# A new plan for layer two's weight pairs inside layer one of a retention and two-MoE kernel

## The chip, the cores and the metric

One core of a Trainium2 chip runs the whole program in one launch. The metric is the device time of an execution in microseconds; the median of three runs of the kernel before is 853.76 us (853.73 to 854.74).

## The reference, cut to what matters

```python
scores = scale * np.matmul(q, k.transpose(0, 1, 3, 2))          # 4 x 8 heads, 576 x 576, head 64
ret = scores * Dmat[None]                                        # decay gamma ** (i - j), causal
x = np.matmul(ret, v).transpose(0, 2, 1, 3).reshape(2304, 512)
h = x @ w_in;   g = np.maximum(h, 0) + alpha * np.minimum(h, 0)  # layer one, d_ff 2048
x = g @ w_out
h = x @ w_in2;  g = h * (1 / (1 + np.exp(-1.702 * h)))           # layer two, d_ff 2048
return g @ w_out2
```

The weights arrive as 64-bit floats, two 32-bit words each, and are turned into 32-bit floats on the chip. Each operand of a matmul is split into a rounded high part and the rest (hi and lo), and three products (hi hi, hi lo, lo hi) replace one.

## The kernel before, in words

There are three stages. Retention comes first (L228 to L346 of the kernel). Layer one follows: the 2304 tokens are cut into five chunks (`CH`, four of 512 columns, number 4 of 256), and the work is a list of 80 steps, numbered 0 to 79 here. One step takes one chunk and one tile of 128 hidden features: `mm1` (L394) makes h with 12 matmuls, ScalarE and VectorE make g from it (`activate`: two ACT passes L404 and L405, one DVE pass L406), `split` writes g's high part on ACT (L84, by `copy`) and its low part on DVE (L87, by `sub`) into `gsf`, and `mm2` (L437) adds the product with the second weight into four banks of PSUM, acc0 to acc3. TensorE's order is mm1(i), mm2(i - 2), mm1(i + 1), and so on. Steps 0 to 31 do chunks 0 and 1 in five blocks, 32 to 47 chunk 2, 48 to 63 chunk 4, 64 to 79 chunk 3. When a chunk ends, its four acc banks are copied out (L458 on DVE, L84 on ACT), and the next chunk's first mm2 writes the same banks. The next chunk's input is loaded (L376, tile xf) and split into x ahead of the change by `x_load` and `x_split`.

Layer two follows in three rounds. It is a scheme with 7 products of blocks in place of 8, a product being one unit (L558, 6 matmuls of 384 columns). Before round 0 it needs x2 (`x2_load`, `x2_steps`: four sums, seven splits for each of k = 0 and 1) and `ws` (split by `r_split` from `rw`). Its 16 weight tiles are converted in eight pairs (j = 0 to 7) during layer one, which `pair_words` plans. A pair is

- for each of its two tiles: the load of raw words (L110, two halves of 512 KB), `w_abs` (ACT, L114), `w_clamp` (DVE, L118 and L121), `w_top` (DVE, L128), `w_low` (DVE, L135), which turn tile raw into tile cv;
- `sums1` and `sums2` (DVE, L465, four sums of 128x256 each);
- `r_store`, five DMAs into rg in DRAM (L178 to L182);
- for seven blocks in three groups: `b_hi` (ACT, L84, rounds a half of the block in place), `b_lo` (DVE, L197), `b_store` (two DMAs into sg in DRAM, L201).

The places of tiles make waits. There are two buffers of cv and two of raw. `b_hi` overwrites what `r_store` reads, so it waits until that DMA has landed. `w_abs` of the next pair overwrites what `b_store` reads, so it waits for that. All DMAs are issued by SP, in program order.

The order is written by hand: every piece of work is put on a list with a time (`at`), and `run_to` emits what is due between the pieces of a step. All engines run what they were given in order. The times of the pairs are microseconds since the start of layer one; `tick` turns them into steps by what TensorE takes for a step without waits.

```python
    def tick(us):
        i = max(n for n in range(n_s) if begins[n] <= us)
        return base + i + (us - begins[i]) / (begins[i + 1] - begins[i])
```

Of the kernel before, what the change touches and what calls it, by code (L numbers as in the profile page):

```python
# [7 lines left out]
F32 = mybir.dt.float32  # L8
# [21 lines left out]
R, RN = 3, 384  # L30
# [2 lines left out]
BANK = "abcabcb"  # L33
GSRC = (0, 4, 1, 3, 0, 2, 3)
NG = 5


@with_exitstack
def kernel(
# [12 lines left out]
    nc = tc.nc  # L52
# [5 lines left out]
    def pool(name, bufs, **kw):  # L58
        return ctx.enter_context(tc.tile_pool(name=name, bufs=bufs, **kw))
# [4 lines left out]
    xp = (pool("xp", 1), pool("xq", 1))  # L64
# [16 lines left out]
    sg = [[dram.tile([128, 4, 2, 256], F32, name=f"sg_{i}_{h}") for h in range(2)] for i in range(7)]  # L81
# [10 lines left out]
    def at(time, fn, *args):  # L92
        events.append((time, len(events), fn, args))

    def run_to(time):
        while events and events[0][0] <= time:
            _, _, fn, args = events.pop(0)
            fn(*args)


    wt, raws, cvs, x_t, sums = {}, {}, {}, {}, {}
    both = "p (c n) -> p c n"

    def w_load(key, src, slot):
# [48 lines left out]
    def quarter(j, e, c):  # L153
        return cvs[2, 2 * j + e][:, c * 256:c * 256 + 256]

    def sums1(j, home):
        if home < 2:
            t = cvp.tile([128, 2, 4, 256], F32, tag=f"raw{home}", name="sums")
            t = [t[:, g] for g in range(2)]
        else:  # L160
            t = [xp[0].tile([128, 4, 256], F32, tag=f"x{2 + g}", name="sums") for g in range(2)]
        sums[j] = t
        m = [[quarter(j, e, c) for c in range(2)] for e in range(2)]
        add(t[0][:, 1], m[1][0], m[1][1])
# [19 lines left out]
    def block2(j, i):  # L184
        if i in (1, 2, 4, 5):
            n = {1: 0, 2: 1, 4: 2, 5: 3}[i]
            return sums[j][0][:, n], sums[j][1][:, n]
        e, h, l = {0: (0, 3, 2), 3: (1, 0, 2), 6: (1, 1, 3)}[i]
        return quarter(j, e, h), quarter(j, e, l)
# [7 lines left out]
        nc.vector.tensor_tensor(out=f.bitcast(F32R), in0=f, in1=hi, op=ALU.subtract)  # L197

    def b_store(j, i):
        for c, t in enumerate(block2(j, i)):  # L200
            nc.sync.dma_start(out=sg[i][j // 4][:, j % 4, c], in_=t)  # L201

    def pair_words(j, t0, t1, l0, l1, slots, home):
        for e, (t, ld) in enumerate(((t0, l0), (t1, l1))):
            key = 2, 2 * j + e
            at(tick(ld), w_load, key, w2, slots[e])
            at(tick(ld) + 0.01, w_piece, key, w2, 1)
            for fn, d in ((w_abs, 0.0), (w_clamp, 2.0), (w_top, 3.6), (w_low, 5.2)):
                at(tick(t + d), fn, key)
        t = t1 + 7.8  # L210
        at(tick(t), sums1, j, home)
        at(tick(t + 1.0), r_store, j)
        at(tick(t + 1.6), sums2, j)
        t += 2.0
        for g, blocks in enumerate(((0, 3), (6, 1), (2, 4, 5))):
            for i in blocks:
                at(tick(t + 2.8 * g), b_hi, j, i)
                at(tick(t + 2.8 * g + 2.8), b_lo, j, i)
                at(tick(t + 2.8 * g + 4.2), b_store, j, i)


    ld, r_t, k_t, s_t, sc_t, av_t, xs_t = {}, {}, {}, {}, {}, {}, {}
# [142 lines left out]
    acc = [None]  # L365
# [118 lines left out]
    def x2_load(r, k):  # L484
        for h in range(2):
            if r:
                t = cvp.tile([128, 2, RN], F32, tag="cv", name="xr", bufs=2)
            else:
                t = xp[0].tile([128, 2, RN], F32, tag=f"x{2 * k + h}", name="xr")
            xr[k, h] = t  # L490
            f = t.rearrange("p c n -> p (c n)")
            for c, (c0, c1) in enumerate(CH):
                s0, s1 = max(c0, r * 2 * RN), min(c1, r * 2 * RN + 2 * RN)
                if s0 < s1:
                    nc.sync.dma_start(
                        out=f[:, s0 - r * 2 * RN:s1 - r * 2 * RN],
                        in_=x1[c][:, 2 * h + k, s0 - c0:s1 - c0],
                    )
# [22 lines left out]
    def x2_steps(k, t, step, gap):  # L521
        for i in range(7):
            for phase in range(3):
                at(t + step * i + gap * phase, x2_step, k, i, phase)
# [21 lines left out]
        t = ws["s", n] = wp.tile([128, 4, 2, 256], F32R, tag=f"w{6 + n % 5}", name="ws2")  # L546
        nc.sync.dma_start(out=t.bitcast(F32), in_=sg[i][h])

    def new_bank(what, n):
        tag = {"a": f"acc{n}", "b": "h", "c": f"acc{2 + n}"}[what]  # L550
        t = mps.tile([128, 512], F32, tag=tag, name=tag, bufs=4 if what == "b" else 1)
        return t[:, 0:RN]

    def product(out, pairs, start):
        n = 0
        for w, x in pairs:
            for cw, cx in ((0, 0), (1, 0), (0, 1)):
                nc.tensor.matmul(  # L558
                    out=out, lhsT=w(cw), rhs=x(cx), start=(start and n == 0), stop=True,
                    skip_group_check=True,  # L560
                )
                n += 1

    def unit1(j, i):
        b = BANK[i]
        new = i < 3 or b == "b"
        if new:
            bank[b] = new_bank(b, j % 2)
        w = ws[2 * j + i // 4][:, :, i % 4]
        product(  # L570
            bank[b],
            [
                (lambda c, k=k: w[:, c, k * 128:k * 128 + 128], lambda c, k=k: xblk(i, k, c))
                for k in range(2)
            ],
            new,
        )
# [100 lines left out]
    for m, t in enumerate(pace):  # L678
        d = 0.75 if m < 3 else 0.5
# [3 lines left out]
    for i in range(n_a):  # L683
        b = PAIRS[i][0]
# [7 lines left out]
    with tc.manual_schedule():  # L692
# [47 lines left out]
        n1 = base + n_s  # L740
        homes = {c: xp[c] for c in range(2)}
        for n, (_, c, m0, _) in enumerate(BLOCKS[N_FIRST:], 1):
            homes[c] = xp[n % 2]
            for k in range(NK):
                t = starts[c, m0] - (4 if n == 1 else 6) + (0.9 if n == 1 else 1.3) * k
                at(t - 1.6, x_load, c, k)
                at(t, x_split, c, k, xp[n % 2])
        for c, n, t in ((0, 0, 17), (1, 1, 25.5), (0, 2, 30)):
# [14 lines left out]
        )):  # L763
            pair_words(j, *plan)
        x2_steps(0, n1 - 7.2, 0.4, 0.5)
        at(n1 - 8.4, x2_load, 0, 0)
        x2_steps(1, n1 - 2.4, 0.4, 0.5)
        at(n1 - 3.2, x2_load, 0, 1)
        for n in range(3):
            at(n1 - 1.5, r_load, n)  # L770
        for n in range(2):
# [24 lines left out]
        for r in range(R):  # L796
# [41 lines left out]
        for u in range(R * 2 * NU):  # L838
            r, v = divmod(u, 2 * NU)
            if v < NU:  # L840
                unit1(*divmod(v, 7))
            else:
                unit2(v - NU)
            run_to(u + 1)
# [60 lines left out]
```

## Time and profile before

| | |
|---|---|
| median of 3 runs | 853.76 us |
| the profiled execution, its own time | 855.07 us |
| its span in the profile | 853.3 us |
| retention, about | 0 to 83.6 us |
| layer one, first mm1 to the last mm2 | 83.6 to 495.97 us |
| layer two, first unit | 498.59 us |
| DVE and ACT busy, share of the span | 74% and 54% |

Times inside the profile count from the start of its span. In a timeline row, several instructions of one kind are merged; the bracket at its end is the idle time of the engine ahead of it and what ended it.

### The profile page before, as it was taken

The numbers are of one execution on the slowest core, as the hardware profiler recorded it, in microseconds if no ns is written. First come the engines' busy times: TensorE is split into PE (matmuls) and PEld (weight loads), VectorE is DVE, ScalarE is ACT, GpSimd is POOL, SyncE is SP. The second block draws the span as 40 slices with busy tenths as digits, with TensorE's granted clock in tenths as the row PEclk, the third lists the DMA queues.
The fourth block names the chain that finished last, engine by engine and source line by source line (L and its number), as shares of the span: only waits on it lengthen the run. The fifth ranks groups of instructions, "written<-read, shape, count | busy, mean of one in ns | idle before, by whom it ended". The sixth has DMA issues, their size and how long they took to land.

```text
span 853.3 us, 14011 instructions
## 1 busy us (share of the span) xinstructions
PE 830.4 (97%) x5132; PEld 755.2 (88%) x5132; DVE 633.2 (74%) x1128; ACT 457.9 (54%) x920; POOL 0.2 (0%) x4
## 2 busy tenths in 40 slices
PE   8999999999999999899998989999999999999998
PEld 7888888888888888798786879999999999999998
DVE  2997796777485587666767678779877799677875
ACT  4643665554353445445435566666566566566553
POOL 0000000000000000000000000000000000000000
PEclk8999999999999999899999999999999999999999
DMA  7985742454156563754554544498544787544872
GB/s 264 324 310 184 250 170 99 151 193 173 35 202 214 173 208 101 235 186 136 204 194 140 190 162 128 150 340 293 198 139 130 264 296 268 178 122 173 295 275 81
DMA packets 66548, 166.97 MB, mean 196 GB/s; under 512 B 7600, under 2 KB 33840, under 8 KB 60720
## 3 DMA queue, kind: packets, MB, share of 16 engines
q1 hardware_dynamic: 66480, 166.08, 57.0%
q8 instruction: 40, 0.66, 0.3%
q14 instruction: 28, 0.23, 0.1%
HBM read 128.83 MB, written 37.22 MB: 195 GB/s over the span
## 4 chain that ended last, share of the span: by engine, by line
PE 77%; DVE 9%; DMA 6%; ACT 4%; issue 3%; SPq 1%; DVEq 0%; ACTq 0%
PE acc L558 24%; PE h L558 18%; PE h L394 15%; PE acc L437 15%; PE av L262 3%; DMA raw<-in_w_dram 2%; DMA sg<-cv 2%; DVE sums L465 1%; PE st L262 1%; PE sc L262 1%; DMA rg<-sums 1%; DVE g L406 1%; DVE cv L118 1%; ACT cv L114 1%; DVE cv L128 1%
## 5 line engine op out<-in xcount | busy, mean ns | idle before, releaser
L437 PE MATMUL acc<-gsf,w 128*128 128x512 f32 (+1 forms) x960 | 216.0, 374 | 9.9 <-DVE o L458 5.2
L394 PE MATMUL h<-x,w 128*128 128x512 f32 (+1 forms) x960 | 211.7, 370 | 0.0
L437 PEld LDWEIGHTS acc<-gsf,w 128*128 128x128 f32 x960 | 170.4, 192 | 44.6 <-DVE gsf L87 6.6
L84 ACT ACTIVATE gsf<-g 128x384 fp32r<-128x384 f32 (+2 forms) x248 | 132.8, 543 | 120.0 <-DVE g L406 77.4
L394 PEld LDWEIGHTS h<-x,w 128*128 128x128 f32 x960 | 169.3, 190 | 30.8 <-DVE w L87 0.7
L87 DVE TENSOR_TENSOR gsf<-g,gsf 128x384 fp32r<-128x384 f32 (+2 forms) x248 | 141.5, 580 | 51.2 <-ACT gsf L84 49.7
L558 PE MATMUL acc<-x,ws 128*128 128x384 f32 x576 | 112.2, 336 | 2.6 <-DVE o L458 2.6
L406 DVE SCALAR_TENSOR_TENSOR g<-h,nalpha_sb,g 128x512 f32<-128x512 f32 (+1 forms) x80 | 55.6, 695 | 72.5 <-ACT h L405 72.2
L558 PEld LDWEIGHTS acc<-x,ws 128*128 128x128 f32 x576 | 101.5, 189 | 3.0 <-ACT ws L84 3.0
L558 PE MATMUL acc<-gsf,ws 128*128 128x384 f32 x576 | 101.3, 334 | 0.0
L558 PEld LDWEIGHTS acc<-gsf,ws 128*128 128x128 f32 x576 | 100.0, 188 | 0.0
L558 PE MATMUL h<-x,ws 128*128 128x384 f32 x432 | 87.4, 337 | 0.0
L558 PEld LDWEIGHTS h<-x,ws 128*128 128x128 f32 x432 | 76.8, 190 | 0.0
L558 PE MATMUL h<-gsf,ws 128*128 128x384 f32 x432 | 76.3, 334 | 0.0
L558 PEld LDWEIGHTS h<-gsf,ws 128*128 128x128 f32 x432 | 75.0, 188 | 0.0
L404 ACT ACTIVATE g<-h 128x512 f32<-128x512 f32 (+1 forms) x80 | 43.7, 547 | 49.9 <-PE h L394 49.8
L465 DVE TENSOR_TENSOR tm<-h,tm 128x384 f32<-128x384 f32 x72 | 40.0, 555 | 35.8 <-PE h L558 31.5
L87 DVE TENSOR_TENSOR ws<-rw,ws 128x512 fp32r<-128x512 f32 x96 | 57.0, 616 | 0.0
L465 DVE TENSOR_TENSOR g<-g,g 128x384 f32<-128x384 f32 x93 | 51.4, 553 | 0.7
L84 ACT ACTIVATE ws<-rw 128x512 fp32r<-128x512 f32 x96 | 49.8, 569 | 0.0
L114 ACT ACTIVATE cv<-raw 128x1024 f32<-128x1024 f32 x32 | 36.1, 1128 | 17.5 <-DMA raw<-in_w_dram 13.9
L405 ACT ACTIVATE h<-h 128x512 f32<-128x512 f32 (+1 forms) x80 | 44.0, 550 | 0.0
(70 smaller groups left out, 687.5 us busy)
## 6 DMA issues: line engine op xcount, KB each, us to landing
ws<-sg SPq DMA_DIRECT2D x42, 1024.0 KB, 6.8
raw<-in_w_dram SPq DMA_DIRECT2D x64, 512.0 KB, 4.9
ld<-in_qkv_dram SPq DMA_DIRECT2D x15, 864.0 KB, 6.7
rw<-rg SPq DMA_DIRECT2D x24, 512.0 KB, 3.5
rw<-rg SPq DMA_DIRECT2D x24, 384.0 KB, 3.1
sg<-sums SPq DMA_DIRECT2D x64, 128.0 KB, 2.0
sg<-cv SPq DMA_DIRECT2D x48, 128.0 KB, 3.0
kts<-in_kn_dram SPq DMA_DIRECT2D x16, 256.0 KB, 6.9
```

Of the source, the lines that this page charges most:

```text
L84: return nc.scalar.activation(out=out, in_=in_, func=ACTF.Copy)
L87: return eng.tensor_tensor(out=out, in0=a, in1=b.bitcast(F32), op=ALU.subtract)
L114: nc.scalar.activation(out=cvs[key], in_=raws[key][:, :, 1].bitcast(F32), func=ACTF.Abs)
L118: nc.vector.tensor_scalar(out=f, in0=f, scalar1=F64_MIN, scalar2=F64_MAX, op0=ALU.max, op1=ALU.min)
L262: nc.tensor.matmul(out=out, lhsT=lhsT, rhs=rhs, start=start, stop=stop, skip_group_check=True)
L394: nc.tensor.matmul(out=t, lhsT=w[:, cw, k * 128:k * 128 + 128], rhs=x[:, cx], start=(i == 0), stop=(i == 3 * NK - 1),)
L404: nc.scalar.activation(out=g, in_=t, func=ACTF.Relu)
L405: nc.scalar.activation(out=t, in_=t, func=ACTF.Relu, scale=-1.0)
L406: nc.vector.scalar_tensor_tensor(out=g, in0=t, scalar=nalpha_sb[:, m:m + 1], in1=g, op0=ALU.mult, op1=ALU.add)
L437: nc.tensor.matmul(out=acc[0][d], lhsT=w[:, cw, d * 128:d * 128 + 128], rhs=g[:, cx], start=(m == m0 and i == 0), stop=(m == m1 - 1 and i ...
L465: nc.vector.tensor_tensor(out=out, in0=x, in1=y, op=op)
L558: nc.tensor.matmul(out=out, lhsT=w(cw), rhs=x(cx), start=(start and n == 0), stop=True, skip_group_check=True,)
```

## The change: what it does

It changes the plan's numbers and rules in `pair_words`, the homes of a few tiles, the form of some stores, and the banks of layer two's first pair.

- `PAUSES`: `tick` adds 10, 9 and 11 us to a plan time that reaches 176, 261 and 309 us. Pair work is thus planned around the three ends of chunks. The table of the pairs has new times, for the words (t0, t1) and the loads (l0, l1).
- Inside a pair the steps are closer: the words' pieces at 0, 1.6, 3.0, 4.4 us (0, 2.0, 3.6, 5.2 before), sums at t1 + 6.2 (7.8), the groups of blocks 2.4 us apart (2.8).
- Loads of the next pair's words are planned after `r_store` of the pair before it.
- The sums of pair 4 live in tiles x2 and x3 of pool xq (`home` 3), those of pair 5 in raw1; pair 6 stays in pool xp. x2's raw input `xr` for k = 1 is loaded into x0 and x1, as for k = 0, and no longer into x2 and x3. k = 0 begins 0.8 step earlier, k = 1 1.0 step earlier, and its load 1.2 step earlier.
- Blocks 3 and 6 are stored by one DMA with two runs per partition, and so are blocks 1, 2, 4, 5 where the sums lie in one tile.
- x of chunks 4 and 3 is split 4.4 steps (6 before) ahead of their first step, 0.9 step apart (1.3).
- In pair j = 0 of round 0, layer two's banks a and c come from the four buffers of h and no longer from acc.

```diff
+PAUSES = ((176, 10), (261, 9), (309, 11))
...
-            t = [xp[0].tile([128, 4, 256], F32, tag=f"x{2 + g}", name="sums") for g in range(2)]
+            t = [xp[home - 2].tile([128, 4, 256], F32, tag=f"x{2 + g}", name="sums") for g in range(2)]
...
     def b_store(j, i):
-        for c, t in enumerate(block2(j, i)):
-            nc.sync.dma_start(out=sg[i][j // 4][:, j % 4, c], in_=t)
+        dst = sg[i][j // 4][:, j % 4]
+        if i in (3, 6):
+            f = cvs[2, 2 * j + 1].rearrange("p (a b n) -> p a b n", a=2, b=2)
+            nc.sync.dma_start(out=dst, in_=f[:, :, i // 6])
+        elif i and j in whole:
+            nc.sync.dma_start(out=dst, in_=whole[j][:, :, {1: 0, 2: 1, 4: 2, 5: 3}[i]])
...
-            for fn, d in ((w_abs, 0.0), (w_clamp, 2.0), (w_top, 3.6), (w_low, 5.2)):
+            for fn, d in ((w_abs, 0.0), (w_clamp, 1.6), (w_top, 3.0), (w_low, 4.4)):
...
-                t = xp[0].tile([128, 2, RN], F32, tag=f"x{2 * k + h}", name="xr")
+                t = xp[0].tile([128, 2, RN], F32, tag=f"x{h}", name="xr")
...
-        tag = {"a": f"acc{n}", "b": "h", "c": f"acc{2 + n}"}[what]
+        tag = "h" if ring else {"a": f"acc{n}", "b": "h", "c": f"acc{2 + n}"}[what]
...
-                t = starts[c, m0] - (4 if n == 1 else 6) + (0.9 if n == 1 else 1.3) * k
+                t = starts[c, m0] - (4 if n == 1 else 4.4) + 0.9 * k
...
+            for begin, length in PAUSES:
+                us += length if us >= begin else 0
...
-            (320, 334, 312, 327, (1, 0), 2), (349, 357, 328, 342, (1, 0), 2),
+            (296, 307, 289, 300, (0, 1), 2), (322, 328, 304.5, 316, (0, 1), 2),
...
-        x2_steps(0, n1 - 7.2, 0.4, 0.5)
-        at(n1 - 8.4, x2_load, 0, 0)
-        x2_steps(1, n1 - 2.4, 0.4, 0.5)
-        at(n1 - 3.2, x2_load, 0, 1)
+        for k in range(2):
+            at(n1 - 9.0 + 4.6 * k, x2_load, 0, k)
+            x2_steps(k, n1 - 8.0 + 4.6 * k, 0.4, 0.5)
```

In the changed kernel the lines after the inserted ones have moved: L465 is L473 there, L406 is L414, L458 is L466, L87 is L88, L135 is L136, L110 is L111, L178 to L182 are L180 to L184.

SP, about step 47 to 49, where pair 3's results are stored and pair 4's words loaded (rg_101 belongs to pair 4). Before:

```order
L110 DMA raw<-in_w_dram 128x1024 x2
L178 DMA rg_100<-cv 128x256
L179 DMA rg_100<-cv 128x256
L180 DMA rg_100<-cv 128x256
L181 DMA rg_100<-sums 128x512
L182 DMA rg_100<-sums 128x512
L201 DMA sg_0_105<-cv 128x256 x2
L201 DMA sg_0_111<-cv 128x256 x2
```

and now:

```order
L180 DMA rg_100<-cv 128x256
L181 DMA rg_100<-cv 128x256
L182 DMA rg_100<-cv 128x256
L183 DMA rg_100<-sums 128x512
L184 DMA rg_100<-sums 128x512
L111 DMA raw<-in_w_dram 128x1024 x2
L210 DMA sg_0_105<-cv 128x256 x2
L205 DMA sg_0_111<-cv 128x2x256
```

The 1 MB load has moved from ahead of the five stores into rg to behind them, and so ahead of the stores into sg; block 3's store is one DMA.

VectorE (DVE) at the end of chunk 2, from g of step 47 to the copy of acc0 and acc2 (COPY o). Before:

```order
L406 SCALAR_TENSOR_TENSOR g<-h,nalpha_sb,g 128x512
L87 TENSOR_TENSOR gsf<-g,gsf 128x512
L197 TENSOR_TENSOR cv<-cv 128x256 x2
L406 SCALAR_TENSOR_TENSOR g<-h,nalpha_sb,g 128x256
L197 TENSOR_TENSOR cv<-cv 128x256
L197 TENSOR_TENSOR sums<-sums 128x256
L87 TENSOR_TENSOR gsf<-g,gsf 128x256
L406 SCALAR_TENSOR_TENSOR g<-h,nalpha_sb,g 128x256
L458 COPY o<-acc_2447 128x512
L458 COPY o<-acc_2449 128x512
```

and now:

```order
L414 SCALAR_TENSOR_TENSOR g<-h,nalpha_sb,g 128x512
L199 TENSOR_TENSOR sums<-sums 128x256 x3
L88 TENSOR_TENSOR gsf<-g,gsf 128x512
L119 TENSOR_SCALAR cv<-cv 128x1024
L122 TENSOR_SCALAR cv<-cv 128x1024
L414 SCALAR_TENSOR_TENSOR g<-h,nalpha_sb,g 128x256
L88 TENSOR_TENSOR gsf<-g,gsf 128x256
L414 SCALAR_TENSOR_TENSOR g<-h,nalpha_sb,g 128x256
L466 COPY o<-acc_2438 128x512
L466 COPY o<-acc_2440 128x512
```

Pair 3's `b_lo` (cv<-cv and sums<-sums) now ends in step 47; only pair 4's first `w_clamp` stands in step 48, and nothing of a pair between it and the copies.

VectorE in step 74, the fullest 512-column step after the change (x, xr, xs belong to `x2_steps`, cv and sums to pair 7). Before:

```order
L118 TENSOR_SCALAR cv<-cv 128x1024
L121 TENSOR_SCALAR cv<-cv 128x1024
L87 TENSOR_TENSOR x_4129<-xr,x_4129 128x384
L128 SCALAR_TENSOR_TENSOR cv<-raw,cv 128x1024
L465 TENSOR_TENSOR xs<-xr 128x384
L406 SCALAR_TENSOR_TENSOR g<-h,nalpha_sb,g 128x512
L135 SCALAR_TENSOR_TENSOR cv<-raw,cv 128x1024
L87 TENSOR_TENSOR x_4148<-xr,x_4148 128x384
L87 TENSOR_TENSOR gsf<-g,gsf 128x512
```

and now:

```order
L122 TENSOR_SCALAR cv<-cv 128x1024
L88 TENSOR_TENSOR x_4109<-xr,x_4109 128x384
L129 SCALAR_TENSOR_TENSOR cv<-raw,cv 128x1024
L473 TENSOR_TENSOR xr<-xs,xr 128x384
L414 SCALAR_TENSOR_TENSOR g<-h,nalpha_sb,g 128x512
L136 SCALAR_TENSOR_TENSOR cv<-raw,cv 128x1024
L88 TENSOR_TENSOR x_4087<-xs,x_4061 128x384
L473 TENSOR_TENSOR xr<-xr,xs 128x384
L473 TENSOR_TENSOR sums<-cv 128x256
L473 TENSOR_TENSOR sums<-sums,cv 128x256
L473 TENSOR_TENSOR sums<-cv 128x256
L473 TENSOR_TENSOR sums<-cv,sums 128x256
```

(One `w_clamp` row stands ahead of these, and gsf 128x512 ends the step.) The four sums and one x2 operation have come into this step from step 75.

## Rows read from the trace of the kernel before

**Rows 1.** The page: busy time by engine, and the granted clock in 40 slices.

```profile
PE 830.4 (97%) x5132; PEld 755.2 (88%) x5132; DVE 633.2 (74%) x1128; ACT 457.9 (54%) x920; POOL 0.2 (0%) x4
...
PEclk8999999999999999899999999999999999999999
```

**Rows 2.** TensorE's timeline, steps 48 to 52: start, length, line, wait ahead.

```profile
339.15 1.60 PE L394 MATMUL h<-x,w 128*128 128x256 f32 x12
...
353.37 2.90 PE L437 MATMUL acc<-gsf,w 128*128 128x256 f32 x12 [3.44 <-DVE o L458]
...
360.40 1.60 PE L394 MATMUL h<-x,w 128*128 128x256 f32 x12
361.84 1.60 PE L437 MATMUL acc<-gsf,w 128*128 128x256 f32 x12
```

**Rows 3.** TensorE's timeline, steps 60 to 67, the change from chunk 4 to 3.

```profile
383.44 1.60 PE L394 MATMUL h<-x,w 128*128 128x256 f32 x12
...
397.67 2.91 PE L394 MATMUL h<-x,w 128*128 128x512 f32 x12
...
410.67 3.01 PE L437 MATMUL acc<-gsf,w 128*128 128x512 f32 x12 [1.73 <-DVE o L458]
413.51 2.88 PE L394 MATMUL h<-x,w 128*128 128x512 f32 x12
416.23 2.88 PE L437 MATMUL acc<-gsf,w 128*128 128x512 f32 x12
```

**Rows 4.** TensorE's timeline, step 74 to layer two's fifth unit.

```profile
458.46 4.09 PE L437 MATMUL acc<-gsf,w 128*128 128x512 f32 x10 [2.67 <-DVE gsf L87]
...
484.14 2.88 PE L394 MATMUL h<-x,w 128*128 128x512 f32 x12
...
498.59 1.62 PE L558 MATMUL acc<-x,ws 128*128 128x384 f32 x6 [2.62 <-DVE o L458]
...
504.40 1.20 PE L558 MATMUL h<-x,ws 128*128 128x384 f32 x6
505.44 1.20 PE L558 MATMUL acc<-x,ws 128*128 128x384 f32 x6
```

**Rows 5.** All engines' timeline ahead of the wait in rows 2 (SPq: DMA issues).

```profile
340.36 0.81 SPq L110 DMA_DIRECT2D raw<-in_w_dram  x2
...
346.99 0.42 ACT L84 ACTIVATE cv<-cv 128x256 fp32r<-128x256 f32 x1 [1.84 <-DMA rg<-cv]
...
348.34 0.42 ACT L84 ACTIVATE sums<-sums 128x256 fp32r<-128x256 f32 x1 [0.93 <-DMA rg<-sums]
...
352.54 1.28 DVE L458 COPY o<-acc 128x512 f32<-128x512 f32 x2
```

**Rows 6.** DMA issues by tiles: count, KB each, median us from issue to landing.

```profile
sg<-sums SPq DMA_DIRECT2D x64, 128.0 KB, 2.0
...
rg<-cv SPq DMA_DIRECT2D x24, 128.0 KB, 5.6
```

**Rows 7.** All engines' timeline ahead of the two waits in rows 4.

```profile
450.52 1.14 ACT L114 ACTIVATE cv<-raw 128x1024 f32<-128x1024 f32 x1 [1.26 <-DMA sg<-cv]
...
486.80 0.56 DVE L465 TENSOR_TENSOR xr<-xr 128x384 f32<-128x384 f32 x1 [4.42 <-DMA xr<-x]
...
497.75 1.28 DVE L458 COPY o<-acc 128x512 f32<-128x512 f32 x2
```

**Rows 8.** VectorE by line and form, 260 to 500 us: busy us, mean ns | idle before.

```profile
L406 DVE SCALAR_TENSOR_TENSOR g<-h,nalpha_sb,g 128x512 f32<-128x512 f32 x31 | 23.2, 748 | 30.4 <-ACT h L405 30.4
...
L135 DVE SCALAR_TENSOR_TENSOR cv<-raw,cv 128x1024 int32<-128x1024 int32 x14 | 17.1, 1220 | 0.2
L465 DVE TENSOR_TENSOR sums<-cv 128x256 f32<-128x256 f32 x28 | 11.7, 418 | 0.0
L121 DVE TENSOR_SCALAR cv<-cv 128x1024 int32<-128x1024 int32 x14 | 9.7, 694 | 0.5
L87 DVE TENSOR_TENSOR x<-xr,x 128x384 fp32r<-128x384 f32 x12 | 6.6, 553 | 0.0
```

More of the change, by code (lines that the diff above doesn't have):

```diff
@@ L98, in run_to @@
             fn(*args)
-    wt, raws, cvs, x_t, sums = {}, {}, {}, {}, {}
+    wt, raws, cvs, x_t, sums, whole = {}, {}, {}, {}, {}, {}
     both = "p (c n) -> p c n"
@@ L158, in sums1 @@
             t = cvp.tile([128, 2, 4, 256], F32, tag=f"raw{home}", name="sums")
+            whole[j] = t
             t = [t[:, g] for g in range(2)]
         else:
-            t = [xp[0].tile([128, 4, 256], F32, tag=f"x{2 + g}", name="sums") for g in range(2)]
+            t = [xp[home - 2].tile([128, 4, 256], F32, tag=f"x{2 + g}", name="sums") for g in range(2)]
         sums[j] = t
@@ L199, in b_store @@
     def b_store(j, i):
-        for c, t in enumerate(block2(j, i)):
-            nc.sync.dma_start(out=sg[i][j // 4][:, j % 4, c], in_=t)
+        dst = sg[i][j // 4][:, j % 4]
[4 more added lines that the diff above has]
+            nc.sync.dma_start(out=dst, in_=whole[j][:, :, {1: 0, 2: 1, 4: 2, 5: 3}[i]])
+        else:
+            for c, t in enumerate(block2(j, i)):
+                nc.sync.dma_start(out=dst[:, c], in_=t)
     def pair_words(j, t0, t1, l0, l1, slots, home):
@@ L207, in pair_words @@
             at(tick(ld) + 0.01, w_piece, key, w2, 1)
-            for fn, d in ((w_abs, 0.0), (w_clamp, 2.0), (w_top, 3.6), (w_low, 5.2)):
+            for fn, d in ((w_abs, 0.0), (w_clamp, 1.6), (w_top, 3.0), (w_low, 4.4)):
                 at(tick(t + d), fn, key)
-        t = t1 + 7.8
+        t = t1 + 6.2
         at(tick(t), sums1, j, home)
-        at(tick(t + 1.0), r_store, j)
-        at(tick(t + 1.6), sums2, j)
-        t += 2.0
+        at(tick(t + 0.9), r_store, j)
+        at(tick(t + 1.5), sums2, j)
         for g, blocks in enumerate(((0, 3), (6, 1), (2, 4, 5))):
             for i in blocks:
-                at(tick(t + 2.8 * g), b_hi, j, i)
-                at(tick(t + 2.8 * g + 2.8), b_lo, j, i)
-                at(tick(t + 2.8 * g + 4.2), b_store, j, i)
+                at(tick(t + 1.8 + 2.4 * g), b_hi, j, i)
+                at(tick(t + 4.2 + 2.4 * g), b_lo, j, i)
+                at(tick(t + 5.4 + 2.4 * g), b_store, j, i)
     ld, r_t, k_t, s_t, sc_t, av_t, xs_t = {}, {}, {}, {}, {}, {}, {}
@@ L547, in s_load, with new_bank @@
         nc.sync.dma_start(out=t.bitcast(F32), in_=sg[i][h])
-    def new_bank(what, n):
-        tag = {"a": f"acc{n}", "b": "h", "c": f"acc{2 + n}"}[what]
-        t = mps.tile([128, 512], F32, tag=tag, name=tag, bufs=4 if what == "b" else 1)
+    def new_bank(what, n, ring=False):
+        tag = "h" if ring else {"a": f"acc{n}", "b": "h", "c": f"acc{2 + n}"}[what]
+        t = mps.tile([128, 512], F32, tag=tag, name=tag, bufs=4 if tag == "h" else 1)
         return t[:, 0:RN]
@@ L562, in product, with unit1 @@
                 n += 1
-    def unit1(j, i):
+    def unit1(r, j, i):
         b = BANK[i]
@@ L567, in unit1 @@
         if new:
-            bank[b] = new_bank(b, j % 2)
+            bank[b] = new_bank(b, j % 2, r + j == 0)
         w = ws[2 * j + i // 4][:, :, i % 4]
@@ L840 @@
             if v < NU:
-                unit1(*divmod(v, 7))
+                unit1(r, *divmod(v, 7))
             else:
```

6 rows, old and new, of the table i are left out of this document.

## The prediction

> **What bounds the kernel now.** I read the page first: TensorE (PE) is busy 97% of the span, DVE 74%, ACT 54%, and past its first slice the granted clock shows one dip, in the 17th of 40 slices, 341 to 363 us [rows 1]. So TensorE sets the end, and a change that adds no matmul and removes none can only win back what TensorE loses to waits and to a lower clock. Then I went down TensorE's timeline through layer one and compared starts with the undisturbed pace. That pace is 1.44 us for 12 matmuls of 256 columns (360.40 to 361.84, [rows 2]), 2.72 us for 12 of 512 (413.51 to 416.23, [rows 3]) and 1.04 us for a unit of layer two (504.40 to 505.44, [rows 4]). Up to step 48 the starts keep it. From there to layer two's fifth unit they do not, and the losses fall into six places:
>
> - A, chunk 2 to 4: 339.15 to 360.40 is 21.25 us; two mm1 of 256 with two mm2 of 512, then two steps of 256, should take 2 x 4.16 + 2 x 2.88 = 14.08. Lost: 7.17 [rows 2].
> - B, the last four steps of chunk 4: 383.44 to 397.67 is 14.23 against 4 x 2.88. Lost: 2.71 [rows 3].
> - C, chunk 4 to 3: 397.67 to 413.51 is 15.84 against 2 x 4.16 + 5.44. Lost: 2.08 [rows 3].
> - D, steps 67 to 79: 413.51 to 484.14 is 70.63 against 12 x 5.44 [rows 3, 4]. Lost: 5.35.
> - E, the end of layer one: 484.14 to 498.59 is 14.45 against 4 x 2.72. Lost: 3.57 [rows 4].
> - F, layer two's first four units: 498.59 to 504.40 is 5.81 against 4.16. Lost: 1.65 [rows 4].
>
> Together 22.53 us. Part of it is clock: behind the wait of 3.44 us, 12 matmuls of 256 took 2.90 us, where 1.60 is usual, so TensorE ran at 1.2 GHz and not 2.4; behind the wait of 1.73 us they took 3.01, where 2.88 is usual, so the clock held [rows 2, 3]. From layer two's fifth unit on TensorE has no gaps. So 22.53 us is the most that the change can win, and 855.07 - 22.53 = 832.54 us the floor for the profiled execution; the median shown lies 1.31 us under that execution, so the floor is 831.2 us against the median.
>
> **The change part by part.**
>
> *The end of chunk 2 (A).* TensorE waits 3.44 us for DVE's copy of the acc banks [rows 2]. DVE is late because ACT was: at 340.36 SP issued 1 MB of raw words, behind that the stores into rg, and ACT's b_hi stood 1.84 us and then 0.93 us until they had landed, with g's passes and the copies queued behind it [rows 5]. Two things change. A store of 128 KB into rg takes 5.6 us to land (the load is ahead of it), one of the same size into sg 2.0 us [rows 6]; with the load behind the five stores I take 2.0 for rg too. And pair 3's sums come at plan time 242.5 + 6.2 = 248.7 and not 246 + 7.8 = 253.8, so that in the new order its last b_lo is in step 47, ahead of g of step 48. What is left between g and the copies in step 49 is nothing of a pair. So A goes from 7.17 to 0.3. Bounds: 0, and 7.17 if ACT is late for another reason.
>
> *The end of chunk 4 (B and C).* Here the new plan puts more on DVE. Steps 60 to 63 now hold four splits of x, all words of pair 5 and its first sums. With 1.22 us for each of w_top and w_low, 0.69 for each pass of w_clamp, 0.42 for a 128x256 sum or low part, 0.75 for a 512-column g or split [rows 8] (a 256-column g or split of g taken at 0.42): step 60 has 3 x 0.42 + 2 x 0.75 + 2 x 0.69 + 1.22 + 2 x 0.42 = 6.2, step 61 2.8, step 62 4.2, step 63 3.7, in all 16.9 us in 11.52 us of TensorE. The means hold some overlap of neighbours, so this is an upper bound. The slack: mm2(i) starts five groups after mm1(i) does, 7.2 us; mm1 itself takes 1.44 of them and the way to gsf's low part five passes of 0.42 (two on ACT, one on DVE, one on each again, all taken at a DVE row's 0.42), so 3.7 us can be late. 5.4 over less 3.7 is 1.7 us of waiting if no DMA comes late. I take 1.5 for B, near that end because hand-overs between engines are left out. Behind it mm1 has 512 columns again and each step 1.28 us more, so C's wait of 1.73 us for the copies [rows 3] goes to 0: the copies follow g of step 65 with no sums between. Bounds for B: 0 and, if x's k = 2 waits for the stores of pair 4's sums (they now lie in xq's x2, x3, where that x goes) for as long as a store behind a load takes, 1.7 + 5.6 - 2.0 = 5.3.
>
> *Steps 67 to 79 (D).* The wait of 2.67 us for gsf of step 72 [rows 4] goes back to ACT's w_abs of pair 7, which stood 1.26 us for block 0's store into sg to land, ahead of g in the same queue [rows 7]. Before, that store is planned at 334 + 7.8 + 2.0 + 4.2 = 348.0 and w_abs at 349; now 348.6 and 352, and w_abs stands behind g of step 72. That wait should go. But x2's first part comes earlier and meets pair 7: step 73 has 7.0 us of DVE by [rows 8], step 74 9.2 (2 x 0.69 + 2 x 1.22 + 4 x 0.55 + 4 x 0.42 + 2 x 0.75), step 75 5.7, in all 21.9 in 16.32 us, 5.6 over. The slack of a 512-column step is, in the same way, 5 x 2.72 - 2.72 - 5 x 0.75 = 7.1 us, of which the wait for pair 6's stores uses some at step 72. I take 1.2 us for what comes of it, between 0 and the whole 5.35.
>
> *The end of layer one and the first units (E, F).* The wait of 2.62 us [rows 4] is for DVE's copy at 497.75; DVE was behind because xr for k = 1 landed late, 4.42 us of idle DVE [rows 7]. It is now loaded 1.2 steps, 6.5 us, earlier, more than that wait, and a and c of the first pair no longer need the acc banks at all. So E and F lose 0.3 each. What the ring of four costs: pair 0's third b (its seventh unit) takes the buffer that a had, and waits for ACT's reads of a. No row shows that wait; the nearest is the 2.62 us that it replaces. a's last product is the fourth unit, three units (3.1 us) ahead, so I take it within F's 0.3.
>
> *The rest.* 28 DMAs fewer (blocks 3 and 6 of eight pairs, four blocks of three pairs) only shorten SP's issue; the same bytes move. Below nothing there is no gain to be had, since layer two and retention keep their order. Pairs 1 to 3 come closer together and fill DVE more: step 44, the fullest, has 5 x 0.42 + 2 x 0.69 + 2 x 1.22 + 2 x 0.75 = 7.4 us and the two behind it 5.7 and 6.1, in all 2.9 over three steps of 5.44, covered by the 7.1 us of slack; without that cover the 2.9 us come on top.
>
> Sum: 855.07 - 22.53 + 0.3 + 1.5 + 0 + 1.2 + 0.3 + 0.3 = 836.1 us for the profiled execution, and 1.31 less, **834.8 us**, against the median.
>
> **A rule that speaks against it.** The 1 MB load that leaves the rg stores' front is now at the front of the sg stores, and w_abs of the next pair waits for those. The gap of 5.6 to 2.0 us in [rows 6] is what a load ahead has cost a store. The Trainium skill (DMA: Bandwidth & Descriptors, section "Queues, rings and completion order") says that each DMA engine takes the descriptors of a queue in ring order; by it the cost is passed on whole, 3.6 us at each pair. By the plan the sg stores come 4.5 us behind the rg stores, so that most of the load should be through.
>
> **The rivals.**
>
> 1. *The load's delay moves to sg.* w_abs is 3.6 us later at every pair. In steps of 512 the slack of 7.1 us takes it, except at steps 72 to 75, where DVE's 5.6 us already use it: D stays at 5.35. 834.8 + 5.35 - 1.2 = 839.0. For it: [rows 6], and w_abs did wait for sg before [rows 7]. Against: 4.5 us between. Chance 0.13.
> 2. *DVE binds at the end of chunk 4.* B costs its upper bound of 5.3 us, and at such a wait the clock falls, for which F's 1.65 is the price: 834.8 + 5.3 + 1.65 - 1.5 = 840.3. For it: 16.9 us of DVE in 11.52. Against: the means overlap. Chance 0.14.
> 3. *Slower: two buffers of cv are too few for the closer pairs.* Pair 1's block 0 is stored at plan time 204.1 and pair 2's w_abs comes at 206.5. ACT stands there for the landing less 2.4 us, and TensorE feels it when that passes the slack, so from a landing of 9.5 us on. At 14 us it costs 4.5 us at each of seven boundaries: 31.5 - 22.53, about 863 us. It decides (slower than before) from 9.5 + 22.53 / 7 = 12.7 us. [Rows 6] has 5.6 us behind a load. Chance 0.05.
> 4. *It doesn't do what it says*: the waits stay, as other late work takes ACT's place ahead of the copies. 853.8. Against: the order at A. Chance 0.02.
>
> **How the numbers follow.** Forecast 0.66 (its own range 831.2 to 838.5), rivals 0.13, 0.14, 0.05, 0.02. A measurement of this kernel tells 0.2% from no change, 1.7 us. All but rivals 3 and 4 are faster: 0.93. Same 0.02, slower 0.05. The range goes from just below the floor, 831.0, to rivals 1 and 2 together, 834.8 + 4.15 + 5.45 = 844.4.
>
> **What would show it.** Right: no PE wait over 1 us at the changes of chunk 2 and 4, PEclk 9 in all slices between, ACT's idle for rg under 4 us, the first unit of layer two right behind the last mm2. B and D wrong: PE waits for gsf at steps 60 to 62 or 74 to 75 of more than 2 us, with the clock at 1.2 GHz behind them. Rival 1: ACT's w_abs idle for DMA sg over 10 us in all. The forecast is wrong as a whole if TensorE's starts from step 48 to layer two's first unit take more than 150 us (159.4 before; 138.6 without loss).

## The result, and the profile after

The changed kernel takes 845.83 us (median of 4 runs, 845.12 to 846.14) against 853.75 (4 runs, 853.46 to 854.74): a ratio of 0.9904 (95% interval 0.9887 to 0.9921), 7.9 us less. I had forecast 834.8 and a range of 831.0 to 844.4. So the sign was right, and the time lies 1.4 us above the range.

The page of the changed kernel answers [rows 1]: engine, busy time, share of the span, instructions.

```profile
span 844.0 us, 13950 instructions
PE 824.5 (98%) x5132; PEld 749.9 (89%) x5132; DVE 634.0 (75%) x1128; ACT 458.0 (54%) x920; POOL 0.2 (0%) x4
PEclk9999999999999999999999999999999999999999
```

TensorE is still the bound, with waits left. Its timeline answers [rows 2 to 4]: start, length, line, wait ahead.

```profile
89.38 2.88 PE L445 MATMUL acc<-gsf,w 128*128 128x512 f32 x12
...
320.88 2.88 PE L402 MATMUL h<-x,w 128*128 128x512 f32 x12
326.48 3.26 PE L445 MATMUL acc<-gsf,w 128*128 128x512 f32 x12 [2.72 <-ACT gsf L85]
...
333.86 2.56 PE L445 MATMUL acc<-gsf,w 128*128 128x512 f32 x10 [0.95 <-DVE gsf L88]
...
341.70 2.11 PE L402 MATMUL h<-x,w 128*128 128x256 f32 x12
...
353.54 1.67 PE L445 MATMUL acc<-gsf,w 128*128 128x256 f32 x12 [0.66 <-DVE o L466]
...
357.93 1.60 PE L402 MATMUL h<-x,w 128*128 128x256 f32 x12
...
380.97 1.60 PE L402 MATMUL h<-x,w 128*128 128x256 f32 x12
...
389.46 0.50 PE L445 MATMUL acc<-gsf,w 128*128 128x256 f32 x2 [0.88 <-ACT gsf L85]
391.08 1.46 PE L445 MATMUL acc<-gsf,w 128*128 128x256 f32 x10 [1.12 <-DVE gsf L88]
...
396.48 2.91 PE L402 MATMUL h<-x,w 128*128 128x512 f32 x12
...
410.40 2.88 PE L402 MATMUL h<-x,w 128*128 128x512 f32 x12
...
465.36 4.03 PE L445 MATMUL acc<-gsf,w 128*128 128x512 f32 x10 [2.45 <-DVE gsf L88]
...
480.11 2.88 PE L402 MATMUL h<-x,w 128*128 128x512 f32 x12
...
490.99 7.47 PE L566 MATMUL h<-x,ws 128*128 128x384 f32 x42
498.30 1.20 PE L566 MATMUL acc<-x,ws 128*128 128x384 f32 x6
```

The starts of steps 45, 48, 52, 60, 64, 67 and 79 and of layer two stand in these rows. Taking the same pace as in the prediction, TensorE loses, in us (Z, steps 45 to 47, is new: 341.70 - 320.88 = 20.82 against 16.32):

| | Z | A | B | C | D | E | F | sum |
|---|---|---|---|---|---|---|---|---|
| before | 0 | 7.17 | 2.71 | 2.08 | 5.35 | 3.57 | 1.65 | 22.53 |
| forecast | 0 | 0.3 | 1.5 | 0 | 1.2 | 0.3 | 0.3 | 3.6 |
| after | 4.50 | 2.15 | 3.99 | 0.16 | 4.43 | 0 | 0.03 | 15.26 |

The gain in the table is 7.27 us. The two profiled executions differ by 9.3 in span; 1.96 of that is retention, which was not changed (mm2(0) starts at 89.38, at 91.34 before; over the executions below at 89.1 to 91.9).

What ends the waits is on ACT. Its waits from 230 to 500 us: engine, line, waited for, then us in total, times, longest.

```profile
ACT cv L85 <- DVE sums L473: 30.1, 8, 6.0
ACT cv L115 <- DMA sg<-cv: 12.5, 4, 4.9
ACT cv L115 <- DMA sg<-sums: 5.7, 1, 5.7
```

L115 is `w_abs`: it stands 18.2 us for stores into sg, 1.7 before. The waits for rg are gone (15.2 before, 8.2 of it for cv and 7.0 for sums). This is the stretch ahead of Z in the timeline of all engines, with pair 2's stores on SP and pair 3's first `w_abs` on ACT:

```profile
315.00 0.32 SPq L184 DMA_DIRECT2D rg<-sums  x1
315.41 0.91 SPq L111 DMA_DIRECT2D raw<-in_w_dram  x2
316.13 0.73 ACT L85 ACTIVATE cv<-cv 128x256 fp32r<-128x256 f32 x2 [5.98 <-DVE sums L473]
...
316.89 1.90 SPq L210 DMA_DIRECT2D sg<-cv  x2
...
318.89 1.01 ACT L85 ACTIVATE sums<-sums 128x256 fp32r<-128x256 f32 x3
319.00 0.75 DVE L414 SCALAR_TENSOR_TENSOR g<-h,nalpha_sb,g 128x512 f32<-128x512 f32 x1 [0.22 <-ACT h L413]
...
324.79 1.12 ACT L115 ACTIVATE cv<-raw 128x1024 f32<-128x1024 f32 x1 [4.88 <-DMA sg<-cv]
325.80 0.62 ACT L85 ACTIVATE gsf<-g 128x512 fp32r<-128x512 f32 x1
326.45 0.69 DVE L88 TENSOR_TENSOR gsf<-g,gsf 128x512 fp32r<-128x512 f32 x1 [6.04 <-ACT gsf L85]
```

SP issues the 1 MB load at 315.41 and block 0's store from 316.89 on, 1.48 us behind it; of that row's two DMAs the second, with the low half, goes out at 318.47 and takes 6.2 us to land. `w_abs` can write its tile only at 324.79, when that store has landed. g of step 43 is ready at 319.75 (the row of L414), but its split stands behind `w_abs` on ACT until 325.80, DVE's half of it behind ACT, and TensorE behind both. The landing times answer [rows 6]: count, KB each, median us from issue to landing.

```profile
raw<-in_w_dram SPq DMA_DIRECT2D x64, 512.0 KB, 5.1
...
sg<-sums SPq DMA_DIRECT2D x40, 128.0 KB, 3.3
...
rg<-cv SPq DMA_DIRECT2D x24, 128.0 KB, 1.8
...
sg<-cv SPq DMA_DIRECT2D x16, 128.0 KB, 5.0
```

rg lands in 1.8 us instead of 5.6, but sg's 128 KB stores take longer: 3.3 us from sums instead of 2.0, 5.0 from cv instead of 3.0. (The rows of sg hold fewer stores than before, as the merged ones have left them; the 16 from cv are block 0's alone.) The other large waits have the same form: `w_abs` idle 3.43 us ahead of 299.64 (pair 2, taken up by the slack), 3.14 ahead of 383.70 (pair 5, then B), 5.70 ahead of 447.93 (pair 7, then D; the view names a store from sums there, but the wait is gone with block 0 out of the way, in e2).

### The profile page after: what moved, and what is told of

Same layout as the page of the kernel before. It is cut to its first block, busy times and chain, and to the rows that moved or that the text cites. A ratio compares the mean times of both kernels' runs of the same rounds, so it can differ in the third digit from the quotient of the medians.

```text
span 844.0 us, 13950 instructions
## 1 busy us (share of the span) xinstructions
PE 824.5 (98%) x5132; PEld 749.9 (89%) x5132; DVE 634.0 (75%) x1128; ACT 458.0 (54%) x920; POOL 0.2 (0%) x4
## 4 chain that ended last, share of the span: by engine, by line
PE 81%; DVE 8%; DMA 5%; ACT 2%; issue 2%; SPq 1%; DVEq 0%; ACTq 0%
PE acc L566 23%; PE h L566 18%; PE acc L445 17%; PE h L402 17%; PE av L270 3%; DVE sums L473 1%; PE st L270 1%; DMA xf<-x 1%; PE sc L270 1%; DVE cv L136 1%; DMA raw<-in_w_dram 1%; DMA sg<-sums 1%; DVE cv L129 1%; DMA sg<-cv 1%; DVE g L414 1%
## 5 line engine op out<-in xcount | busy, mean ns | idle before, releaser
L88 DVE TENSOR_TENSOR gsf<-g,gsf 128x384 fp32r<-128x384 f32 (+2 forms) x248 | 141.8, 580 | 58.7 <-ACT gsf L85 58.0
L414 DVE SCALAR_TENSOR_TENSOR g<-h,nalpha_sb,g 128x512 f32<-128x512 f32 (+1 forms) x80 | 55.6, 695 | 68.5 <-ACT h L413 68.3
L566 PE MATMUL acc<-x,ws 128*128 128x384 f32 x552 | 106.8, 334 | 0.0
L566 PEld LDWEIGHTS acc<-x,ws 128*128 128x128 f32 x552 | 96.7, 188 | 0.0
L566 PE MATMUL h<-x,ws 128*128 128x384 f32 x456 | 90.3, 334 | 0.0
L566 PEld LDWEIGHTS h<-x,ws 128*128 128x128 f32 x456 | 80.1, 188 | 0.1
L473 DVE TENSOR_TENSOR tm<-h,tm 128x384 f32<-128x384 f32 x73 | 40.5, 555 | 33.2 <-PE h L566 28.9
L88 DVE TENSOR_TENSOR ws<-rw,ws 128x512 fp32r<-128x512 f32 x96 | 56.9, 616 | 1.1 <-ACT ws L85 1.1
L473 DVE TENSOR_TENSOR g<-g,g 128x384 f32<-128x384 f32 x93 | 51.5, 554 | 0.7
L115 ACT ACTIVATE cv<-raw 128x1024 f32<-128x1024 f32 x32 | 36.1, 1129 | 24.6 <-DMA sg<-cv 12.5
```

Of the source, the lines that this page charges most:

```text
L88: return eng.tensor_tensor(out=out, in0=a, in1=b.bitcast(F32), op=ALU.subtract)
L115: nc.scalar.activation(out=cvs[key], in_=raws[key][:, :, 1].bitcast(F32), func=ACTF.Abs)
L414: nc.vector.scalar_tensor_tensor(out=g, in0=t, scalar=nalpha_sb[:, m:m + 1], in1=g, op0=ALU.mult, op1=ALU.add)
L566: nc.tensor.matmul(out=out, lhsT=w(cw), rhs=x(cx), start=(start and n == 0), stop=True, skip_group_check=True,)
```

## The experiments

Theory 1: the load's delay has passed from the rg stores to block 0's store into sg, and `w_abs` stands for that with g queued behind it. Theory 2: the closer plan leaves `w_abs` too little time, load or no load. Theory 3: DVE has too much work in the full steps. Each ratio below is to runs of the kernel before on the same occasion, with medians from 851.82 to 852.79 us.

**The load behind the sg stores (e1_load_behind_sg).**

```diff
-(206.5, 212.5, 194, 201, ...), (226.5, 232.5, 214.5, 221, ...)
+(206.5, 212.5, 194, 204.3, ...), (226.5, 232.5, 214.5, 224.3, ...)
...
-(274.5, 280.5, 257, 268.5, ...) ... (322, 328, 304.5, 316, ...)
+(274.5, 280.5, 257, 271.8, ...) ... (322, 328, 304.5, 318.8, ...)
```

> The changed kernel with the second load of pairs 2, 3, 5 and 7 issued behind the stores of blocks 0 and 3 into sg (and no longer between the rg stores and them). Theory 1 (the 1 MB load ahead of the sg stores makes w_abs stand): ACT's idle ahead of w_abs for DMA sg falls from 18 us to under 6; the loss of steps 45 to 47 (4.50 us) falls to about 1, that at the end of chunk 4 (3.99) to 2, that of steps 67 to 79 (4.43) to 2; about 840 us. Theory 2 (the plan leaves too little time between block 0's store and the next w_abs, whatever stands in the queue): the idle stays over 12 us, and so do the losses; 845 us. Theory 3 (DVE has too much work in steps 44, 60 to 63 and 73 to 75 whatever ACT does): the idle falls, TensorE's losses stay within 1 us of what they are; 845 us.

835.5 us, ratio to before 0.9798 (0.9776 to 0.982). ACT's waits for sg, and how long block 0's stores take to land:

```profile
ACT cv L115 <- DMA sg<-cv: 7.7, 4, 3.7
...
ACT cv L115 <- DMA sg<-sums: 2.1, 1, 2.1
...
sg<-cv SPq DMA_DIRECT2D x16, 128.0 KB, 1.9
```

Block 0's stores land in 1.9 us instead of 5.0. The idle falls to 9.8 us (I had set under 6), Z to 0.86, D to 0. B keeps 3.34: there ACT now stands for x of the next chunk (3.40 us for xf, whose load is behind the moved one, and 2.38 for sums' stores). Four numbers of the plan give 9 to 10 us, more than theory 1 had set. That is theory 1 in the main; theory 3 falls, and theory 2 holds at most for what is left.

**Block 0 out of the way (e2_block0_apart).** `b_hi` and `b_lo` of block 0 write to gsf's columns 3072 to 3584, unused in layer one.

```diff
 def b_hi(j, i):
+    if i == 0: copy(gsf[:, 3072:3328], f)
 def b_lo(j, i):
+    if i == 0: sub(nc.vector, gsf[:, 3328:3584], f, gsf[:, 3072:3328])
 def b_store(j, i):
+    elif i == 0: nc.sync.dma_start(out=dst, in_=gsf 3072:3584 as (2, 256))
```

> The changed kernel with block 0's high and low part written to 512 columns of gsf that layer one leaves unused, and stored from there, so that w_abs of the next pair waits for no sg store of block 0; loads where the change has them. Theories 1 and 2: no idle of ACT ahead of a pair's first w_abs for DMA sg; losses of steps 45 to 47 at most 1 us, end of chunk 4 about 2, steps 67 to 79 about 2; 839 to 840 us. Theory 3: losses as in the changed kernel, 845 us.

831.87 us, ratio 0.9754 (0.9736 to 0.9772), faster than any of the three theories had it. TensorE's timeline over steps 45 to 48:

```profile
322.29 2.88 PE L411 MATMUL h<-x,w 128*128 128x512 f32 x12
325.01 2.88 PE L454 MATMUL acc<-gsf,w 128*128 128x512 f32 x12
...
333.17 2.88 PE L411 MATMUL h<-x,w 128*128 128x512 f32 x12
335.89 2.88 PE L454 MATMUL acc<-gsf,w 128*128 128x512 f32 x12
338.61 1.60 PE L411 MATMUL h<-x,w 128*128 128x256 f32 x12
```

Every start is 2.72 us behind the last (16.32 us over the six up to step 48). The losses are 0.15 us in all, with DVE's work as in the changed kernel. Theory 3 is dead: the slack does take the full steps. No version here is faster beyond its interval. (The edit also stores block 0 by one DMA; e8 below, with two, takes 833.15.) But the edit takes away two waits, since `b_hi` of block 0 also overwrote what `sums2` reads (30.1 us of idle, now 8.7). So:

**Only the high half apart (e5_hi_apart)**: `b_hi` of block 0 as in e2, the low half and its store as in the changed kernel.

> The changed kernel with block 0's high half alone written to the unused columns of gsf; the low half stays in cv and is stored from there. So block 0's b_hi no longer overwrites what sums2 reads (it waited for that on DVE in the changed kernel, 30.1 us over 8 pairs), but w_abs of the next pair still waits for a store of block 0 into sg. Theory 1 (w_abs waiting for sg is what costs): w_abs for sg stands 8 us or more, the losses of steps 45 to 47 and at the end of chunk 4 keep over half of their size, 841 to 845 us. Rival (b_hi waiting for DVE's sums is what costs): that wait falls below 10 us, the losses fall to under 2 us in all, 832 to 835 us.

844.63 us, ratio 0.9908 (0.9876 to 0.994); losses 15.59 us. From ACT's waits, and TensorE's at Z:

```profile
ACT cv L85 <- DVE sums L477: 13.8, 6, 4.2
ACT cv L115 <- issue: 11.2, 2, 6.1
ACT cv L115 <- DMA sg<-cv: 10.3, 3, 6.2
...
328.41 5.49 PE L449 MATMUL acc<-gsf,w 128*128 128x512 f32 x12 [3.62 <-ACT gsf L85]
```

The idle for sums falls to 13.8 us. `w_abs` stands 21.5: 10.3 for sg, and 11.2 in two stands, at pairs 2 and 7, for which the view finds no releaser ("issue") and where it stands for sg in the changed kernel. At Z ACT stands 4.17 us for the sums (5.98 in the changed kernel) and 6.20 for the store (4.88), and TensorE's wait grows from 2.72 to 3.62. The wait for the store is what costs, not that for the sums.

**`w_abs` 3 us later (e9_w_abs_later).**

```diff
-(206.5, ...), (226.5, ...) ... (274.5, ...) ... (322, ...)
+(209.5, ...), (229.5, ...) ... (277.5, ...) ... (325, ...)
```

> The changed kernel with the first words (w_abs, w_clamp, w_top, w_low) of pairs 2, 3, 5 and 7 planned 3 us later; loads, stores and all else as changed. On ACT that puts w_abs behind the next passes of g or gsf, and not ahead of them; the stores into sg land when they landed. Theory 1 (ACT stands in w_abs with g's passes queued behind it): the idle for DMA sg falls from 18 us to about 6, TensorE's losses from 15.3 to about 7, 838 to 841 us. Rival (DVE's work is what is late; now the words of a pair's two tiles come 3 us closer together and it is later still): TensorE's losses stay or grow, 844 to 850 us.

835.37 us, ratio 0.9786 (0.9762 to 0.981); idle for sg 6.0 us, losses 5.04, half of them at D (2.51). ACT at Z:

```profile
314.41 0.73 ACT L85 ACTIVATE cv<-cv 128x256 fp32r<-128x256 f32 x2 [5.11 <-DVE sums L473]
...
318.09 0.62 ACT L85 ACTIVATE gsf<-g 128x512 fp32r<-128x512 f32 x1
...
321.82 1.12 ACT L115 ACTIVATE cv<-raw 128x1024 f32<-128x1024 f32 x1 [1.64 <-DMA sg<-cv]
```

The load stands where the change has it; `w_abs`, with DVE's three passes on the same tile, is behind g's next passes on ACT, and Z loses nothing, though ACT still stands 5.11 us for the sums. So the place in ACT's order is as good a handle as the queue, and theory 2 has its share: the loss needs both a late store and a `w_abs` planned only 2.4 to 3.4 us behind it, ahead of g.

**The loads ahead of rg again (e3_load_ahead_rg, e12_block0_load_ahead_rg)**, once with block 0 in cv and once apart.

```diff
-(206.5, 212.5, 194, 201, ...), (226.5, 232.5, 214.5, 221, ...), (249, 260, 241, ...)
+(206.5, 212.5, 194, 198.2, ...), (226.5, 232.5, 214.5, 218.2, ...), (249, 260, 238.3, ...)
...
-(274.5, 280.5, 257, 268.5, ...), (296, 307, 289, ...), (322, 328, 304.5, 316, ...)
+(274.5, 280.5, 257, 265.7, ...), (296, 307, 286.2, ...), (322, 328, 304.5, 312.7, ...)
```

> The changed kernel with the loads put ahead of the rg stores again (pairs 2, 3, 5, 7: the second load; 4 and 6: the first), as in the kernel before, all else as changed. Theory 1: the stores into rg land late, ACT's b_hi stands for DMA rg some 2 us at each of four or more pairs, w_abs for sg less than 8 us in all; 844 to 849 us, with a part of the loss back at the end of chunk 2. Theory 2: w_abs waits as in the changed kernel, 846 us. Theory 3: 845 to 846 us, losses where they are.

> As e2_block0_apart, but with the loads ahead of the rg stores again, as in e3_load_ahead_rg. This asks whether the load's new place is worth anything once w_abs no longer waits for block 0's store. Theory (it is: behind the load the rg stores land late, b_hi of block 6 stands for them with g's passes behind it): ACT's idle for DMA rg is 12 us or more, TensorE loses 5 us or more, above all at steps 45 to 52, 837 us or more. Rival (the slack takes it, as b_hi stands only 2 to 3 us at a time): TensorE loses under 2 us, 832 to 833 us.

847.99 us (0.9946, 0.9927 to 0.9965) and 847.19 us (0.9935, 0.9914 to 0.9956). ACT's waits in the second:

```profile
ACT cv L85 <- DMA rg<-cv: 19.6, 5, 4.7
...
ACT sums L85 <- DMA rg<-sums: 3.8, 4, 1.0
```

`w_abs` stands for sg no more in either; `b_hi` stands for rg, 15.7 and 23.4 us, and TensorE loses 16.12 and 14.66. Theory 1 holds in both, and in the second by more than I expected. With the new plan the four cases are:

| us | block 0 in cv | block 0 apart |
|---|---|---|
| load ahead of rg | 847.99 | 847.19 |
| load behind rg | 845.83 | 831.87 |

Either remedy alone shows 0.8 or 2.2 us (0.9 and 3.6 by the ratios), both together 16.

**The kernel before, one part at a time.** e10_before_load_behind_rg moves its six loads behind the rg stores (206 to 207.2, 230 to 231.2, 253 to 255.2 and so on), e6_before_block0_apart puts its block 0 apart, e4_end_alone gives it the change's last part alone:

```diff
+t = xp[0].tile([128, 2, RN], F32, tag=f"x{h}", name="xr")
+for k in range(2):
+    at(n1 - 9.0 + 4.6 * k, x2_load, 0, k)
+    x2_steps(k, n1 - 8.0 + 4.6 * k, 0.4, 0.5)
+tag = "h" if ring else ...
```

> The kernel before with one part of the change alone: the load that stood ahead of the rg stores of pairs 1 to 6 (second load of pairs 2, 3 and 7, first load of 4 to 6) is issued behind them, and so ahead of the stores into sg. Theory 1 (the load's delay is passed on to whatever store is behind it): ACT's idle for DMA rg falls from 15.2 us to under 4, that of w_abs for DMA sg grows from 1.7 to over 8; 849 to 855 us, no gain beyond 3 us. Rival (my forecast's step at the end of chunk 2: the load ahead of rg was what cost there, and behind them it is through by the time sg is stored): rg's idle falls, sg's stays under 3, the loss at the end of chunk 2 falls from 7.17 to under 2; 846 us or less.

> The kernel before with both halves of block 0 written to the unused columns of gsf, plan, loads and all else as before. Theory (before the change the stores into rg, not those of block 0 into sg, were what ACT stood for): the losses at the end of chunk 2 (7.17) and at the change from chunk 4 to 3 (2.08) stay; w_abs of pair 7 no longer stands, so that of steps 67 to 79 falls by some 2 us; 850 to 853 us. Rival (block 0's place was the bound before as well): 845 us or less.

> The kernel before with the part at its end alone: xr of k = 1 in x0 and x1 and loaded earlier, x2's steps at the changed times, first banks from h's ring; the plan of the pairs as before. Theory: the losses at the end of layer one (3.57) and in the first units (1.65) go, all others stay: 853.75 - 5 = 848.7 us. Rival: x2's first part meets pair 7, whose words come at steps 72 to 76 here, and the loss of steps 67 to 79 grows by 3 to 5 us: 852 to 854 us.

e10: 855.77 us, ratio 1.0039 (1.0018 to 1.0061), 0.4% slower than before. Of its ACT waits:

```profile
ACT cv L114 <- DMA sg<-cv: 14.7, 6, 4.4
...
ACT cv L84 <- DMA rg<-cv: 2.6, 1, 2.6
ACT sums L84 <- DMA rg<-sums: 1.2, 1, 1.2
```

rg's 15.2 us have become sg's 14.7. A falls from 7.17 to 1.98, as the rival had it, but D grows from 5.35 to 10.30: ACT stands 4.40 us ahead of 421.25 and TensorE 4.11 behind it. e6: 849.65 us, 0.9973 (0.9957 to 0.9988), losses 18.49; D falls to 1.38, A keeps 5.74 and C grows to 4.00, and ACT's wait for rg grows from 15.2 to 22.4, so block 0's place alone was not the bound before. e4: 850.02 us, 0.9967 (0.9947 to 0.9988); E and F are gone, and D grows to 7.62, by 2.3 us: its theory and half of its rival. (B shows 4.23 there, 1.5 more than before, with nothing edited near it; what moved it stays open, as each of the two kernels has one trace.)

**Two small parts, on e2's kernel.** e7_block0_acc_banks takes layer two's first banks from acc again (`new_bank(b, j % 2)`), e8_block0_single_stores stores every block with two DMAs.

> As e2_block0_apart, but layer two's first pair takes its banks a and c from acc, as before the change. Theory: the first unit waits for the copy of acc behind the last mm2, 1.3 us of copy and some hand-over: 1.5 to 2.6 us more than e2_block0_apart, 833.4 to 834.5 us; the other losses stay at nothing. Rival (the earlier xr load alone takes that wait away): under 0.5 us more, 832 us.

> As e2_block0_apart, but every block is stored by two DMAs of 128 KB, as before the change. Theory: 36 more DMA issues at 0.4 us on SP, none of them waited for: within 1 us of e2_block0_apart, 831 to 833 us. Rival (SP's queue is then late for stores and loads that ACT waits for): a wait for DMA of over 2 us in steps 45 to 63, 834 us or more.

831.33 us (0.9746, 0.9718 to 0.9774) and 833.15 us (0.9775, 0.9751 to 0.9799). In e7 the first unit follows the last mm2 with no wait, so my theory there falls: beside the earlier load of xr the ring banks bring nothing, and E and F went with that load. e8's interval overlaps e2's, and its losses are 1.25 us: nothing or a microsecond for the merged stores.

**The changed kernel once more (e11_changed_again).**

> The changed kernel as it is, on the same chip as the two others, to see what its losses at each place are in another execution. If they are the kernel's and not one execution's, steps 45 to 47, chunk 4's end and steps 67 to 79 lose 4 to 5 us each again, and the time is 843 to 846 us.

846.4 us, ratio 0.9911 (0.9887 to 0.9936). Z 4.32, A 1.32, B 3.87, C 0.17, D 4.42: the losses are the kernel's, place by place.

## Why the prediction was wrong, by its own steps

- **The step that failed** is the one under the rule that spoke against the change: "By the plan the sg stores come 4.5 us behind the rg stores, so that most of the load should be through." The load itself goes out behind the last rg store, and block 0's two DMAs 1.48 and 3.06 us behind the load, of which a half takes 5.1 us to land (4.9 before). With it Rival 1 was priced too low: its wait came as described (18.2 us, where I had set 10 as its sign), but I let the slack of 7.1 us take it everywhere but at D. 839.0 was the price, 845.83 the time.
- **The slack** was counted for DVE's work alone, as if g's split could go as soon as g is there. At Z it stands behind `w_abs` in ACT's order and comes when the store has landed, 6.05 us after g was ready (319.75 to 325.80). So "the rest", costed at nothing with 2.9 us of DVE work as its only risk, cost 4.50. That ACT also stood 5.98 us for the sums ahead of it is not what used the slack up: in e9 it stood 5.11 and Z lost nothing, in e5 4.17 and TensorE waited longer. DVE's full steps were indeed covered: in e2 they cost nothing.
- **A**: the cause named was right and went (rg's idle 15.2 to 0). What is left, 2.15, comes from Z's wait, behind which DVE has no gap until 343 us, and from one of 1.03 us at pair 4's `w_abs`; 0.04 in e2 and e9.
- **B**, 3.99 for 1.5: not DVE's 16.9 us of work, but `w_abs` 3.14 and xf 2.44 us late; 0.04 in e2.
- **D**, 4.43 for 1.2: `w_abs` of pair 7 did not come free as reckoned from plan times. It stood 5.70 us, DVE got g's half 5.53 us late and ran without a gap from 450.02 to 465, and that is when its 5.6 us too many counted. 0 in e1 and e2.
- **C, E, F**: right within 0.3. For E and F the ring banks deserved no credit.
- **The floor** of 831.2 was right: e2 reaches 831.87. The 150 us from step 48 to layer two that were to show the forecast wrong were not reached, if only just (149.29), as Z lies ahead of step 48, where I had looked for nothing.

The Trainium skill's rule that each DMA engine takes a queue's descriptors in ring order (DMA: Bandwidth & Descriptors, section "Queues, rings and completion order") agrees with these runs: the delay of the load stays in the queue and goes to whatever is behind it. ACT stood 15.2 us for rg before, and 14.7 for sg in e10, where rg lands in 1.8 us. I had cited the rule, and had given its rival 0.13.

## What to carry to other kernels

When a transfer is moved out of one waiter's way, find who waits for the next thing in that queue, and take that wait away in the same step: here either remedy alone gave 1 to 4 us and both together 16. Slack that is reckoned from busy time doesn't cover a stand: what is queued behind a waiting instruction on an engine that runs in order starts when the transfer has landed, however early its own input was there. So look at what stands ahead of the critical work in its engine's order before DVE's work is weighed against the slack. A tile that a store reads is in use until the store has landed; look for a spare place for what is stored last before the whole order is planned anew.

## What the runs showed of the hardware

Whether the clock falls behind a wait differs between executions of one program. The wait of D is 2.45 us in the first execution of the changed kernel and 2.46 in e11's; 10 matmuls behind it took 4.03 us in the first and 2.56 in the other. In windows around it (start and end, length, busy time of PE, PEld, DVE, ACT and POOL with instructions, granted clock, DMA share, GB/s), the first execution has

```profile
462.00:471.00 9.00, 6.55 (x23) 4.97 (x22) 7.57 (x19) 3.88 (x10) 0.00 (x0) 0.81 0.34 120
```

and e11's, for Z's wait and for D's:

```profile
326.00:334.00 8.00, 5.87 (x18) 4.19 (x18) 5.59 (x10) 4.85 (x9) 0.00 (x0) 0.79 0.40 132
465.00:473.00 8.00, 5.66 (x24) 4.35 (x24) 6.56 (x17) 3.90 (x10) 0.00 (x0) 1.00 0.38 135
```

A mean of 0.81 or 0.79 is a stretch partly at 1.2 and partly at 2.4 GHz; with 1.00 it was at 2.4 throughout. At Z it was the other way round: 2.72 us of idle and 12 matmuls in 3.26 us in the first execution, 2.13 us and 4.87 in e11's. So one wait of some 2.5 us cost 0 to 2 us beside its own length, and what decided it no run here tells.
